# First-layer tiles of one chunk each, and the first weights ahead of the second chunk's data

## Chip, core and metric

The kernel runs on one NeuronCore of a Trainium2 chip. The metric is the device time of one execution in microseconds (us); the time before is 581.92 us, the median of 3 runs (579.84 to 582.04).

## What is computed

A scan attention over 4 batches, 8 heads, 768 positions, head size 32 and state size 16, then two feed-forward layers on the 3072 tokens of 256 features that come out of it. The scan keeps a state per batch and head; within a chunk it is a masked product of C, B and the decays:

```python
M = einsum(C, B) * L                      # L: decays between positions i >= j
y = einsum(M, x) + einsum(C, state) * decay_to_i
state = decay_full * state + sum(B * x * decay_from_j)
...
h = max(max(x @ w1, x @ w2), x @ w3)      # 256 -> 768
x = h @ w_out                             # 768 -> 256
gate = 1 / (1 + exp(-(x @ w_gate)))       # 256 -> 1536
out = gate * (x @ w_val) @ w_out2         # 1536 -> 256
```

## The kernel before, in words

The sequence is cut into 8 chunks of `CH` = 96 positions. A chunk of all 4 batches is `CP` = 384 tokens. One attention step (`attention`, L269) handles 4 of the 32 (batch, head) units of one chunk, so a chunk takes 8 steps and the whole scan 64. A step is a generator with stages: score matmuls into a PSUM tile (L280 or L283), the product with the decays into `mt` (L288 on GpSimd, L295 on VectorE; for even steps from 4 on L291 on ScalarE and L292 on GpSimd), then the matmuls into `y` (L301). After four steps half a chunk is split into `xt_hi` and `xt_lo` (L310, L312) and the state is transposed into the next chunk's `xs` (L316). Steps 0 to 15 (`FIRST`, the "masked" ones) use fp32 tables with a mask made on ScalarE (L275), and their score matmuls are fp32; later steps use bf16 splits of the tables (`split_bc`, L238, with the products `bi` and `cs`). `decay` (L227) runs two scans on VectorE for each pair of steps; `load_decay` (L211) fetches the data for it, 388 KB per pair, into one of 4 buffers.

The feed-forward matmuls work on tiles of `TT` = 512 tokens: for each tile t and each of 6 blocks m of 128 hidden features, `layer` (L415) makes 3 up-projections of 6 matmuls each (fp32 as hi and lo parts: 3 products for 2 halves of 256 features), and `down` (L356) follows one block later with 6 matmuls. A block is therefore 24 matmuls of up to 512 columns, each with a weight load of its own. The stages `most` and `hidden` (L392, L386) evict: a copy (L395, ScalarE), two maxima (L397, L399, VectorE), the hi cast (L388, ScalarE) and the lo part (L390, GpSimd). `psu` has three PSUM banks, shared by up-projections and scores.

Weights come as 64-bit floats. `load_weights` (L121) issues two transfers of 256 KB per piece on SP's queue (the second part of a second-layer piece: one), and `decode` (L130) turns a piece into hi and lo parts: three ScalarE instructions (L141, L143, L144), two VectorE (L148, L150), a cast on ScalarE (L155) and a subtraction on GpSimd (L157). The first layer has 12 pieces. `BEHIND` says how many pieces follow the issue of decay n.

The order: the prologue (L431 to L456) issues the first loads and traces `START` = 12 attention steps; then the first layer runs tile by tile, and `slot_end` (L463) traces further steps so that `need(t + 1)` of them are done before tile t + 1. Before the change need is 12, 24, 32, 44, 56, 64. The first-layer output of tile 5 is followed by the second layer's (tile, block) list. `tc.issue_after(i)` puts the instructions of its block behind i on i's engine. Each engine executes its queue in order; a scheduler of the compiler fixes that order beforehand from simulated times. All transfers are issued by SP. Per chunk there are 768 KB of x and B (`load_x`, L219), a table of 448 KB (L241 or L443) and, from chunk 2 on, 1344 KB of products (L252).

Of the kernel before, what the change touches and what calls it, by code (L numbers as in the profile page):

```python
# [7 lines left out]
F32 = mybir.dt.float32  # L8
F32R = mybir.dt.float32r
# [9 lines left out]
CH = 96  # L19
# [4 lines left out]
NT = NB * S  # L24
TT = 512
NTT = NT // TT
DM = NH * D
KD = DM // 128
FF1, FF2 = 768, 1536
# [8 lines left out]
TERMS = [(0, 0), (0, 1), (0, 2), (1, 0), (1, 1), (2, 0)]  # L38
KT = 16 * len(TERMS)
DEC = 512  # L40
START = 12
FIRST = 2 * NG
MASKED = 8
LEAD = 2
MTS = 5
DECS = 4

BEHIND = {4: 1, 5: 1, 6: 2, 7: 2, 8: 2, 9: 1, 10: 1, 11: 1, 12: 1}


class Pipe:
# [15 lines left out]
def scan_attention_then_ffn(ctx: ExitStack, tc: tile.TileContext, xh, ah, bch, pick, bn, w1, w2, w3,  # L67
# [170 lines left out]
    def split_bc(c):  # L238

        r = awk.tile([128, BW + 384], F32, tag="bc", bufs=1, name=f"bc{c}")  # L240
        sp.dma_start(out=r, in_=bch[:, c])  # L241
        parts = awk.tile([128, 3, BW + 384], BF16, tag="parts", bufs=1, name=f"parts{c}")
        cs[c] = awk.tile([KT, NU, CH], BF16, tag="cs", name=f"cs{c}")
        yield
        for p in range(3):
            with tc.issue_after(evict[0].ins) if c > 2 else ExitStack():
                act.copy(parts[:, p], r)
            for k, (dst, cols) in enumerate(((bi[c % 2], slice(0, BW)),
                                             (cs[c], slice(BW, BW + 384)))):
                for t, pr in enumerate(TERMS):  # L250
                    if pr[k] == p:
                        sp.dma_start(  # L252
                            out=dst[16 * t:16 * t + 16].rearrange("n (g q) i -> n g (q i)", q=4),
                            in_=parts[:, p, cols])
            if p < 2:
                pool.tensor_tensor(out=r, in0=r, in1=parts[:, p], op=ALU.subtract)
            yield splits if p == 2 else None
# [6 lines left out]

    def need(t):

        return 4 * -(-(t + 1) * TT // (2 * CH))

    def attention(k, ahead):  # L269

        c, g = steps[k]
        m = mt[k % MTS]
        if k < FIRST:
            ck = cm[:, k % MASKED]
            act.mul(ck.rearrange("p q i -> p (q i)"), bcf[c][:, BW:], pk[:, g:g + 1])  # L275
        ps = psu.tile([128, 4, 128], F32, tag="up", name=f"s{c}_{g}")
        for q in range(4):
            u = 4 * g + q
            if k < FIRST:
                pe.matmul(ps[:, q, 0:CH], bcf[c][:, 128 * q:128 * q + 128], ck[:, q],  # L280
                          start=True, stop=True)
            else:
                pe.matmul(ps[:, q, 0:CH], bi[c % 2][:, u, :], cs[c][:, u, :],  # L283
                          start=True, stop=True)
        for _ in range(ahead + 1):
            yield
        dc = dec[k // 2][:, 4 * (g % 2):4 * (g % 2) + 4]
        pool.tensor_tensor(out=m[:, :, CH:CH + N], in0=bx[c][:, 4 * g:4 * g + 4, :],  # L288
                           in1=dc[:, :, CH:LW].to_broadcast([128, 4, N]), op=ALU.mult)
        if k >= 4 and k % 2 == 0:  # L290
            act.copy(m[:, :, 0:CH], ps[:, :, 0:CH])  # L291
            pool.tensor_tensor(out=m[:, :, 0:CH], in0=m[:, :, 0:CH], in1=dc[:, :, 1:LW],  # L292
                               op=ALU.mult)
        else:
            last[0] = dve.tensor_tensor(out=m[:, :, 0:CH], in0=ps[:, :, 0:CH], in1=dc[:, :, 1:LW],  # L295
                                        op=ALU.mult)
        prepare(k)
        yield
        y = ys[g // 4]
        for q in range(4):  # L300
            pe.matmul(y[32 * q:32 * q + 32, g % 4, 0:CH + N], xs[c][:, 4 * g + q, :], m[:, q, :],  # L301
                      start=True, stop=True)
        if g % 4 == 3:
            yield
            h = g // 4
            o = (c * CP + 2 * CH * h) % RING
            src = y[:, :, 0:CH].rearrange("p (b k) i -> p b k i", k=KD)
            hi, lo = (v[:, :, o:o + 2 * CH].rearrange("p k (b i) -> p b k i", b=2)
                      for v in (xt_hi, xt_lo))
            act.copy(hi, src)  # L310
            yield
            dve.tensor_tensor(out=lo, in0=src, in1=hi.bitcast(F32), op=ALU.subtract)  # L312
            if c + 1 < NC:
                for q in range(4):
                    rows = slice(32 * q, 32 * q + 32)
                    dve.transpose(  # L316
                        out=xs[c + 1][rows, 16 * h:16 * h + 16, :].rearrange(
                            "p (g q) d -> p g q d", q=4)[:, :, q, :],
                        in_=y[rows, :, CH:128])

    def prepare(k):

        c, g = divmod(k, NG)
        if g == 0 and 0 < c < NC - 1:
            load_x(c + 1)
            splits.append(split_bc(c + 1))
        if splits and next(splits[0], None) is splits:
            splits.pop()
        n = k // 2
        if k % 2 == 0:  # L330
            if 5 <= n + 4 < NC * NP:
                load_decay(n + 4, ad)
        elif k < 9:
            decay(n + 1, n == 0)
        else:
            for i in ([n + 1] if k == 9 else []) + [n + 2]:
                if i < NC * NP:
                    with tc.issue_after(last[0].ins) if k > FIRST else ExitStack():
                        decay(i)

    def att_step(ahead=0):
# [12 lines left out]
    acc = {}  # L354

    def down(t, m, mn, w, hl, finish):  # L356
        if m == 0:
            acc[t] = [psos[t % len(psos)].tile([128, TT], F32, tag=f"o{d}", name=f"o{mn}_{t}_{d}")
                      for d in range(KD)]
        first = len(w) - KD  # L360
        for d in range(KD):
            three(acc[t][d], [m], mn, w, lambda k: first + d, lambda k: hl[0], lambda k: hl[1])
        if m == mn - 1:
            pipe.add(finish(t, acc[t]))

    def finish1(t, ps):
        yield
        for d in range(KD):
            act.copy(y1[:, d, t * TT:(t + 1) * TT], ps[d])

    def finish2(t, ps):
        yield
# [39 lines left out]
        chain.tick()  # L412
        pipe.tick()

    def layer(t, m, w, n, stages):  # L415

        o = (t * TT) % RING
        s = tmpp.tile([128, TT], F32, tag="s", bufs=3, name=f"s{n}_{t}_{m}")
        hl = [tmpp.tile([128, TT], F32R, tag=h, name=f"{h}{n}_{t}_{m}") for h in ("hi", "lo")]
        banks = []  # L420
        for j in range(n):
            ps = psu.tile([128, TT], F32, tag="up", name=f"u{n}_{t}_{m}_{j}")
            three(ps, range(KD), KD, w, lambda k: KD * j + k,
                  lambda k: xt_hi[:, k, o:o + TT], lambda k: xt_lo[:, k, o:o + TT])
            banks.append(ps)
            if j == 0:
                chain.add(stages(s, banks, hl))
            yield hl
# [9 lines left out]
    next(store_all, None)  # L438
    load_x(0, slice(0, 16))
    load_decay(1, ah)  # L440
    load_decay(2, ad)
    load_x(0, slice(16, 32))
    sp.dma_start(out=bcf[1], in_=bch[:, 1])  # L443
    load_decay(3, ad)
    load_x(1, slice(0, 16))
    load_decay(4, ad)
    decay(0, clip=True)
# [15 lines left out]

    def slot_end():
        t, s = divmod(slot, slots)
        if t + 1 < NTT:
            goal = need(t) + (need(t + 1) - need(t)) * (s + 1) / (slots - 5)
            while done[0] < min(goal, need(t + 1)):
                for _ in range(2 if t > 1 else 1):
                    att_step(1 if t > 1 else 0)  # L470
        tick()
        weights_tick(t < NTT - 1 or s % 3 == 2)

    for t in range(NTT):
        for m in range(M1):
            for hl in layer(t, m, wt1[m], 3, most):
                slot_end()
                slot += 1
            if pend is not None:
                down(*pend)  # L480
            slot_end()
            slot += 1
            pend = (t, m, M1, wt1[m], hl, finish1)
            if t == NTT - 1 and m == 0:
                actx.close()
                wp2.append(ctx.enter_context(tc.tile_pool(name="wp2", bufs=1)))
                psos.append(ctx.enter_context(tc.tile_pool(name="pso2", bufs=1, space=PSUM)))
                todo += [(piece2, m, part) for m in range(M2) for part in range(2)]
                while todo:
                    load_weights()  # L490
            if t == NTT - 1 and m in (2, 4):
                pipe.add(split_y(m // 2 - 1))


# [1 line left out]
    order += [(t, m) for t in range(2, NTT) for m in range(M2)]  # L496
    for t, m in order:
        eng = pool if t < 2 else dve
        for hl in layer(t, m, wt2[m], 2, lambda s, b, h: gated(s, b, h, eng)):
            tick()  # L500
            slot += 1
            weights_tick(slot % 3 == 2)
# [77 lines left out]
```

## Time and profile before

| | |
|---|---|
| median of the runs | 581.92 us |
| the profiled execution's own time | 582.93 us |
| its span, first to last instruction | 581.1 us |
| first matmul of the first layer | 38.19 us |
| first matmul of its second tile | 91.95 us |
| first matmul of the second layer | 281.42 us |
| busy: TensorE, VectorE, ScalarE, GpSimd | 560.9, 312.7, 260.7, 197.8 us |

The span begins with the first instruction of any engine and ends with the last; the rest of the execution's time lies around it. PE is TensorE's matmuls, PEld its weight loads, DVE VectorE, ACT ScalarE, POOL GpSimd, SP SyncE. Recorded matmuls overlap each other, so the pace of a stream of them is the distance of their starts, not the recorded duration.

### The profile page before, as it was taken

Reading aid. Unit: us, or ns where it says so; the run is one execution under the profiler, and the core shown is the slowest. Engines: PE = TensorE matmul, PEld = TensorE weight load, DVE = VectorE, ACT = ScalarE, POOL = GpSimd, SP = SyncE. Lnnn points to the kernel's source line nnn. Section 1 sums busy time; section 2 is a strip of 40 time slices with the busy share of each in tenths; the row PEclk is TensorE's granted clock in tenths of the full one; section 3 lists DMA queues with packets and bytes.
Section 4 is the critical chain, followed back from the end, with each engine's and each line's share of the span. In section 5 each row is a group of like instructions: output and inputs, shape, how many; then the busy total and the mean of one; then the engine's idle time right before and its main releaser. Section 6 shows DMA issues by size and latency. Waiting matters only on the chain.

```text
span 581.1 us, 8016 instructions
## 1 busy us (share of the span) xinstructions
PE 560.9 (97%) x2992; PEld 448.7 (77%) x2992; DVE 312.7 (54%) x455; ACT 260.7 (45%) x475; POOL 197.8 (34%) x219
## 2 busy tenths in 40 slices
PE   4988799999999999999999999999999999999997
PEld 4766567677777777788888888888888888888885
DVE  3879995655857754345766664243343333333332
ACT  4677645225344333256967675442333233232322
POOL 3566965427556523234665555310000000000000
PEclk9998999999999999999999999999999999999999
DMA  7999876827875800395000000010000001000000
GB/s 243 335 241 259 222 153 111 174 65 134 196 162 142 156 2 0 94 363 195 2 1 2 0 2 0 1 72 1 1 7 30 1 0 38 0 1 36 1 0 36
DMA packets 35366, 50.52 MB, mean 87 GB/s; under 512 B 3456, under 2 KB 24320, under 8 KB 35328
## 3 DMA queue, kind: packets, MB, share of 16 engines
q1 hardware_dynamic: 35328, 50.02, 33.4%
q8 instruction: 23, 0.38, 0.3%
q14 instruction: 15, 0.12, 0.1%
HBM read 38.51 MB, written 3.25 MB: 72 GB/s over the span
## 4 chain that ended last, share of the span: by engine, by line
PE 87%; DMA 6%; DVE 3%; issue 1%; SPq 1%; ACT 1%; POOL 0%; DVEq 0%; ACTq 0%; POOLq 0%
PE u L350 19%; PE u L351 18%; PE u L352 18%; PE o L351 8%; PE o L350 8%; PE o L352 8%; PE s L280 3%; PE y L301 3%; DMA raw_a<-in_w 3%; PE s L283 1%; DMA dec<-in_ah 1%; DMA cs<-parts 1%; DMA raw_a<-in_wo 1%; DVE dec L235 1%; SPq L252 0%
## 5 line engine op out<-in xcount | busy, mean ns | idle before, releaser
L388 ACT CAST hi<-s 128x512 fp32r<-128x512 f32 x108 | 67.1, 621 | 181.1 <-DVE s L406 132.1
L390 POOL TENSOR_TENSOR lo<-s,hi 128x512 fp32r<-128x512 f32 x60 | 80.9, 1348 | 95.3 <-ACT hi L388 92.3
L350 PE MATMUL u<-xt_hi,w_b 128*128 128x512 f32 x288 | 112.0, 389 | 0.0
L351 PE MATMUL u<-xt_lo,w_b 128*128 128x512 f32 x288 | 112.0, 389 | 0.0
L352 PE MATMUL u<-xt_hi,w_b 128*128 128x512 f32 x288 | 112.0, 389 | 0.0
L406 DVE TENSOR_TENSOR s<-u,s 128x512 f32<-128x512 f32 x72 | 49.6, 689 | 103.8 <-PE u L352 101.7
L350 PE MATMUL u<-xt_hi,w_a 128*128 128x512 f32 x216 | 89.1, 413 | 2.9 <-DVE s L399 2.0
L351 PE MATMUL u<-xt_lo,w_a 128*128 128x512 f32 x216 | 85.5, 396 | 0.1
L352 PE MATMUL u<-xt_hi,w_a 128*128 128x512 f32 x216 | 85.0, 394 | 0.0
L352 PEld LDWEIGHTS u<-xt_hi,w_b 128*128 128x128 f32 x288 | 54.1, 188 | 11.3
L350 PEld LDWEIGHTS u<-xt_hi,w_b 128*128 128x128 f32 x288 | 54.1, 188 | 11.2
L351 PEld LDWEIGHTS u<-xt_lo,w_b 128*128 128x128 f32 x288 | 54.0, 188 | 11.2
L235 DVE TENSOR_TENSOR_SCAN dec<-dec,delta 128x388 f32<-128x388 f32 x64 | 57.9, 945 | 1.7 <-DMA dec<-ad 1.5
L351 PE MATMUL o<-lo,w_b 128*128 128x512 f32 x144 | 56.1, 390 | 0.0
L352 PE MATMUL o<-hi,w_b 128*128 128x512 f32 x144 | 56.0, 389 | 0.0
L350 PEld LDWEIGHTS u<-xt_hi,w_a 128*128 128x128 f32 x216 | 41.2, 191 | 14.7 <-DVE s L399 2.5
L390 DVE TENSOR_TENSOR lo<-s,hi 128x512 fp32r<-128x512 f32 x48 | 33.2, 692 | 32.5 <-ACT hi L388 32.4
L352 PEld LDWEIGHTS u<-xt_hi,w_a 128*128 128x128 f32 x216 | 41.1, 190 | 9.1
L351 PEld LDWEIGHTS u<-xt_lo,w_a 128*128 128x128 f32 x216 | 41.1, 191 | 8.3 <-DVE xt_lo L312 0.6
L404 ACT ACTIVATE s<-u 128x512 f32<-128x512 f32 x72 | 43.1, 599 | 3.6 <-PE u L352 3.0
L350 PE MATMUL o<-hi,w_b 128*128 128x512 f32 x144 | 44.4, 390 | 0.1
L397 DVE TENSOR_TENSOR s<-u,s 128x512 f32<-128x512 f32 x36 | 24.8, 688 | 35.7 <-PE u L352 32.8
(60 smaller groups left out, 769.7 us busy)
## 6 DMA issues: line engine op xcount, KB each, us to landing
dec<-ad SPq DMA_DIRECT2D x30, 388.0 KB, 5.2
raw_a<-in_w SPq DMA_DIRECT2D x18, 256.0 KB, 7.2
bi<-parts SPq DMA_DIRECT2D x36, 128.0 KB, 5.3
cs<-parts SPq DMA_DIRECT2D x36, 96.0 KB, 5.2
xs<-in_xh SPq DMA_DIRECT2D x6, 512.0 KB, 4.5
raw_b<-in_wg SPq DMA_DIRECT2D x12, 256.0 KB, 5.8
raw_b<-in_wv SPq DMA_DIRECT2D x12, 256.0 KB, 5.8
raw_b<-in_wo SPq DMA_DIRECT2D x12, 256.0 KB, 5.8
```

The costliest lines, as they stand in the source:

```text
L235: dve.tensor_tensor_scan(out=f, data0=f, data1=delta.rearrange("p u w -> p (u w)"), initial=0.0, op0=ALU.mult, op1=ALU.add)
L280: pe.matmul(ps[:, q, 0:CH], bcf[c][:, 128 * q:128 * q + 128], ck[:, q], start=True, stop=True)
L283: pe.matmul(ps[:, q, 0:CH], bi[c % 2][:, u, :], cs[c][:, u, :], start=True, stop=True)
L301: pe.matmul(y[32 * q:32 * q + 32, g % 4, 0:CH + N], xs[c][:, 4 * g + q, :], m[:, q, :], start=True, stop=True)
L350: pe.matmul(ps, wlo, a_hi(k), start=k == 0, stop=False)
L351: pe.matmul(ps, whi, a_lo(k), start=False, stop=False)
L352: pe.matmul(ps, whi, a_hi(k), start=False, stop=k == kn - 1)
L388: act.copy(hl[0], s)
L390: eng.tensor_tensor(out=hl[1], in0=s, in1=hl[0].bitcast(F32), op=ALU.subtract)
L397: dve.tensor_tensor(out=s, in0=banks[1], in1=s, op=ALU.max)
L404: evict[0] = act.activation(out=s, in_=banks[0], func=AF.Sigmoid)
L406: evict[1] = dve.tensor_tensor(out=s, in0=banks[1], in1=s, op=ALU.mult)
```

## The change

The first layer runs over 7 tiles: four of 384 tokens (a chunk each) and three of 512. `need` becomes 8, 16, 24, 32, 44, 56, 64, and `START` 8. `load_weights` is called once after the load of decay 2 and once after the second chunk's table, so the first piece stands ahead of that table, of decays 3 and 4 and of the second chunk's x; `BEHIND` places the other ten pieces behind decays 4 to 9. Chunk 0's second half of x is issued before decay 2. ScalarE's casts in `split_bc` stand behind its latest eviction for every chunk, and that eviction can now be one of the attention's copies. Scans from step 11 on stand behind the latest mask product. From tile 3 on (before: tile 2) attention steps come in pairs. The second layer keeps its tiles of 512.

```diff
--- before.py
+++ after.py
@@ -24,6 +24,9 @@
 NT = NB * S
 TT = 512
 NTT = NT // TT
+
+TILES = [(CP * c, CP) for c in range(4)] + [(4 * CP + TT * c, TT) for c in range(3)]
+NT1 = len(TILES)
 DM = NH * D
 KD = DM // 128
 FF1, FF2 = 768, 1536
@@ -38,14 +41,14 @@
 TERMS = [(0, 0), (0, 1), (0, 2), (1, 0), (1, 1), (2, 0)]
 KT = 16 * len(TERMS)
 DEC = 512
-START = 12
+START = 8
 FIRST = 2 * NG
 MASKED = 8
 LEAD = 2
 MTS = 5
 DECS = 4
 
-BEHIND = {4: 1, 5: 1, 6: 2, 7: 2, 8: 2, 9: 1, 10: 1, 11: 1, 12: 1}
+BEHIND = {4: 1, 5: 1, 6: 2, 7: 2, 8: 2, 9: 2}
 
 
 class Pipe:
@@ -243,7 +246,7 @@
         cs[c] = awk.tile([KT, NU, CH], BF16, tag="cs", name=f"cs{c}")
         yield
         for p in range(3):
-            with tc.issue_after(evict[0].ins) if c > 2 else ExitStack():
+            with tc.issue_after(evict[0].ins):
                 act.copy(parts[:, p], r)
             for k, (dst, cols) in enumerate(((bi[c % 2], slice(0, BW)),
                                              (cs[c], slice(BW, BW + 384)))):
@@ -264,7 +267,7 @@
 
     def need(t):
 
-        return 4 * -(-(t + 1) * TT // (2 * CH))
+        return 4 * -(-sum(TILES[t]) // (2 * CH))
 
     def attention(k, ahead):
 
@@ -288,7 +291,7 @@
         pool.tensor_tensor(out=m[:, :, CH:CH + N], in0=bx[c][:, 4 * g:4 * g + 4, :],
                            in1=dc[:, :, CH:LW].to_broadcast([128, 4, N]), op=ALU.mult)
         if k >= 4 and k % 2 == 0:
-            act.copy(m[:, :, 0:CH], ps[:, :, 0:CH])
+            evict[0] = act.copy(m[:, :, 0:CH], ps[:, :, 0:CH])
             pool.tensor_tensor(out=m[:, :, 0:CH], in0=m[:, :, 0:CH], in1=dc[:, :, 1:LW],
                                op=ALU.mult)
         else:
@@ -307,7 +310,7 @@
             src = y[:, :, 0:CH].rearrange("p (b k) i -> p b k i", k=KD)
             hi, lo = (v[:, :, o:o + 2 * CH].rearrange("p k (b i) -> p b k i", b=2)
                       for v in (xt_hi, xt_lo))
-            act.copy(hi, src)
+            evict[0] = act.copy(hi, src)
             yield
             dve.tensor_tensor(out=lo, in0=src, in1=hi.bitcast(F32), op=ALU.subtract)
             if c + 1 < NC:
@@ -331,11 +334,12 @@
             if 5 <= n + 4 < NC * NP:
                 load_decay(n + 4, ad)
         elif k < 9:
-            decay(n + 1, n == 0)
+            with tc.issue_after(last[0].ins) if k > 9 else ExitStack():
+                decay(n + 1, n == 0)
         else:
             for i in ([n + 1] if k == 9 else []) + [n + 2]:
                 if i < NC * NP:
-                    with tc.issue_after(last[0].ins) if k > FIRST else ExitStack():
+                    with tc.issue_after(last[0].ins) if k > 9 else ExitStack():
                         decay(i)
 
     def att_step(ahead=0):
@@ -354,8 +358,9 @@
     acc = {}
 
     def down(t, m, mn, w, hl, finish):
+        n = hl[0].shape[1]
         if m == 0:
-            acc[t] = [psos[t % len(psos)].tile([128, TT], F32, tag=f"o{d}", name=f"o{mn}_{t}_{d}")
+            acc[t] = [psos[t % len(psos)].tile([128, TT], F32, tag=f"o{d}", name=f"o{mn}_{t}_{d}")[:, 0:n]
                       for d in range(KD)]
         first = len(w) - KD
         for d in range(KD):
@@ -366,7 +371,8 @@
     def finish1(t, ps):
         yield
         for d in range(KD):
-            act.copy(y1[:, d, t * TT:(t + 1) * TT], ps[d])
+            o, n = TILES[t]
+            act.copy(y1[:, d, o:o + n], ps[d])
 
     def finish2(t, ps):
         yield
@@ -412,16 +418,18 @@
         chain.tick()
         pipe.tick()
 
-    def layer(t, m, w, n, stages):
-
-        o = (t * TT) % RING
-        s = tmpp.tile([128, TT], F32, tag="s", bufs=3, name=f"s{n}_{t}_{m}")
-        hl = [tmpp.tile([128, TT], F32R, tag=h, name=f"{h}{n}_{t}_{m}") for h in ("hi", "lo")]
+    def layer(tile, m, w, n, stages):
+
+        o, size = tile
+        name = f"{n}_{o}_{m}"
+        r = slice(o % RING, o % RING + size)
+        s = tmpp.tile([128, TT], F32, tag="s", bufs=3, name=f"s{name}")[:, 0:size]
+        hl = [tmpp.tile([128, TT], F32R, tag=h, name=f"{h}{name}")[:, 0:size] for h in ("hi", "lo")]
         banks = []
         for j in range(n):
-            ps = psu.tile([128, TT], F32, tag="up", name=f"u{n}_{t}_{m}_{j}")
+            ps = psu.tile([128, TT], F32, tag="up", name=f"u{name}_{j}")[:, 0:size]
             three(ps, range(KD), KD, w, lambda k: KD * j + k,
-                  lambda k: xt_hi[:, k, o:o + TT], lambda k: xt_lo[:, k, o:o + TT])
+                  lambda k: xt_hi[:, k, r], lambda k: xt_lo[:, k, r])
             banks.append(ps)
             if j == 0:
                 chain.add(stages(s, banks, hl))
@@ -438,10 +446,12 @@
     next(store_all, None)
     load_x(0, slice(0, 16))
     load_decay(1, ah)
+    load_x(0, slice(16, 32))
     load_decay(2, ad)
-    load_x(0, slice(16, 32))
+    load_weights()
+    load_decay(3, ad)
     sp.dma_start(out=bcf[1], in_=bch[:, 1])
-    load_decay(3, ad)
+    load_weights()
     load_x(1, slice(0, 16))
     load_decay(4, ad)
     decay(0, clip=True)
@@ -463,17 +473,17 @@
 
     def slot_end():
         t, s = divmod(slot, slots)
-        if t + 1 < NTT:
+        if t + 1 < NT1:
             goal = need(t) + (need(t + 1) - need(t)) * (s + 1) / (slots - 5)
             while done[0] < min(goal, need(t + 1)):
-                for _ in range(2 if t > 1 else 1):
-                    att_step(1 if t > 1 else 0)
+                for _ in range(2 if t > 2 else 1):
+                    att_step(1 if t > 2 else 0)
         tick()
-        weights_tick(t < NTT - 1 or s % 3 == 2)
-
-    for t in range(NTT):
+        weights_tick(t < NT1 - 1 or s % 3 == 2)
+
+    for t in range(NT1):
         for m in range(M1):
-            for hl in layer(t, m, wt1[m], 3, most):
+            for hl in layer(TILES[t], m, wt1[m], 3, most):
                 slot_end()
                 slot += 1
             if pend is not None:
@@ -481,14 +491,14 @@
             slot_end()
             slot += 1
             pend = (t, m, M1, wt1[m], hl, finish1)
-            if t == NTT - 1 and m == 0:
+            if t == NT1 - 1 and m == 0:
                 actx.close()
                 wp2.append(ctx.enter_context(tc.tile_pool(name="wp2", bufs=1)))
                 psos.append(ctx.enter_context(tc.tile_pool(name="pso2", bufs=1, space=PSUM)))
                 todo += [(piece2, m, part) for m in range(M2) for part in range(2)]
                 while todo:
                     load_weights()
-            if t == NTT - 1 and m in (2, 4):
+            if t == NT1 - 1 and m in (2, 4):
                 pipe.add(split_y(m // 2 - 1))
 
 
@@ -496,7 +506,7 @@
     order += [(t, m) for t in range(2, NTT) for m in range(M2)]
     for t, m in order:
         eng = pool if t < 2 else dve
-        for hl in layer(t, m, wt2[m], 2, lambda s, b, h: gated(s, b, h, eng)):
+        for hl in layer((t * TT, TT), m, wt2[m], 2, lambda s, b, h: gated(s, b, h, eng)):
             tick()
             slot += 1
             weights_tick(slot % 3 == 2)
```

## Rows read from the trace of the kernel before

**Rows 1.** section 1 of the page: busy us (share) and instructions

```profile
PE 560.9 (97%) x2992; PEld 448.7 (77%) x2992; DVE 312.7 (54%) x455; ACT 260.7 (45%) x475; POOL 197.8 (34%) x219
```

**Rows 2.** by stage: us; PE, PEld, DVE, ACT, POOL busy; clock, DMA, GB/s

```profile
8.40:38.19 29.79, 27.02 (x186) 22.36 (x186) 24.51 (x39) 17.23 (x31) 13.92 (x22) 1.00 0.94 289
38.19:91.95 53.76, 47.53 (x298) 34.77 (x299) 49.74 (x71) 33.28 (x59) 38.28 (x38) 0.97 0.89 220
91.95:281.42 189.47, 188.73 (x1202) 145.77 (x1201) 107.14 (x176) 79.42 (x144) 88.66 (x99) 1.00 0.56 133
211.14:248.78 37.64, 37.64 (x242) 28.96 (x241) 16.20 (x25) 12.16 (x23) 12.73 (x14) 1.00 0.18 54
248.78:281.42 32.64, 32.64 (x146) 27.03 (x145) 15.82 (x26) 20.66 (x42) 14.22 (x11) 1.00 0.68 229
```

**Rows 3.** waits of PE up to 92 us; then a piece of the chain

```profile
PE s L280 <- DMA y<-in_bch: 6.7, 1, 6.7
PE u L350 <- DVE s L399: 1.6, 1, 1.6
PE s L283 <- DVE s L399: 1.6, 1, 1.6
...
52.93 5.79 DMA raw_a<-in_wo
```

**Rows 4.** timeline of PE: start us, us, instruction, count

```profile
15.14 2.02 PE L280 MATMUL s<-y 128*128 128x96 f32 x8
...
17.63 2.02 PE L280 MATMUL s<-y 128*128 128x96 f32 x8
...
41.79 0.63 PE L352 MATMUL u<-xt_hi,w_a 128*128 128x512 f32 x1
42.22 0.63 PE L350 MATMUL u<-xt_hi,w_a 128*128 128x512 f32 x1
...
43.91 0.39 PE L351 MATMUL u<-xt_lo,w_a 128*128 128x512 f32 x1
44.13 0.39 PE L352 MATMUL u<-xt_hi,w_a 128*128 128x512 f32 x1
44.36 1.02 PE L280 MATMUL s<-y 128*128 128x96 f32 x8
45.17 0.48 PE L350 MATMUL u<-xt_hi,w_a 128*128 128x512 f32 x1
```

**Rows 5.** timeline of PE, then of PEld, around 112 us

```profile
112.12 0.39 PE L351 MATMUL u<-xt_lo,w_a 128*128 128x512 f32 x1
...
111.77 0.19 PEld L350 LDWEIGHTS u<-xt_hi,w_a 128*128 128x128 f32 x1
111.88 0.19 PEld L351 LDWEIGHTS u<-xt_lo,w_a 128*128 128x128 f32 x1
112.12 0.19 PEld L352 LDWEIGHTS u<-xt_hi,w_a 128*128 128x128 f32 x1
```

**Rows 6.** groups of DVE up to 92 us: count | busy us, mean ns

```profile
L235 DVE TENSOR_TENSOR_SCAN dec<-dec,delta 128x388 f32<-128x388 f32 x28 | 25.4, 946 | 1.7 <-DMA dec<-ad 1.5
L148 DVE SCALAR_TENSOR_TENSOR t_a<-raw_a,sg 128x512 int32<-128x512 int32 x12 | 13.3, 1111 | 1.2 <-DMA cs<-parts 1.1
L150 DVE CUSTOM_DVE_ANT_0 r_a<-t_a,r_a 128x1024 uint16<-128x1024 uint16 x12 | 13.1, 1095 | 0.8 <-ACT raw_a L143 0.5
L295 DVE TENSOR_TENSOR mt<-s,dec 128x384 f32<-128x384 f32 x14 | 7.6, 546 | 2.9 <-PE s L280 2.9
L316 DVE STREAM_TRANSPOSE xs<-y 32x128 f32<-32x128 f32 x24 | 7.4, 310 | 0.2
...
L399 DVE TENSOR_TENSOR s<-u,s 128x512 f32<-128x512 f32 x5 | 3.4, 679 | 0.1
```

**Rows 7.** timeline: last first-layer weights, their issue (SP) and last decode (POOL)

```profile
67.86 0.33 SPq L127 DMA_DIRECT2D raw_a<-in_wo  x1
...
85.27 1.28 POOL L157 TENSOR_TENSOR w_a<-r_a,w_a 128x512 fp32r<-128x512 f32 x1 [2.34 <-ACT w_a L155]
```

## Prediction

> **What bounds the kernel now.** I read the busy shares first: TensorE works for 97% of the span [rows 1], so most of what can be won is either TensorE work that gets cheaper or the little time in which it waits. The table by stage comes next. Its edges are the first matmuls of the first layer (38.19 us), of that layer's second tile (91.95), and of the second layer (281.42) [rows 2]. From 91.95 to 281.42 TensorE is busy for 188.73 of 189.47 us: nothing waits there. From 38.19 to 91.95 it is busy for 47.53 of 53.76 us, and VectorE for 49.74, which is 92.5% of the stretch [rows 2]. So during the first tile VectorE's queue is the fullest. The waits and the chain say the same: TensorE stands 1.6 us twice for a VectorE maximum (L399), and behind that the chain runs through weight transfers of 5.79 us and the like [rows 3]: VectorE executes in order, and a decode instruction that is late holds up the eviction behind it. The DMA engines are busy for 0.94 and 0.89 of the two early stretches [rows 2].
>
> One more thing in the rows: TensorE starts slow. Eight masked score matmuls and what follows them repeat every 2.49 us at 15.14; at 44.36 the same eight lengthen the stream by 45.17 - 44.13 - 0.23 = 0.81 us. First-layer matmuls stand 0.43 us apart from 41.79 to 42.22 and 0.22 us apart from 43.91 to 44.13 [rows 4]. These are the two levels, 1.2 and 2.4 GHz. (The clock column shows 1.00 before 43 us; the spacings contradict it there.) TensorE reached the upper level some 5 us after the first layer began. What runs before that costs double.
>
> **The change, part by part.** Everything is counted against the profiled execution: span 581.10 us, its own time 582.93, so 1.83 lie around the span; the median of the runs, 581.92, is 1.0 below it.
>
> *First matmul of the first layer.* Twelve attention steps stand ahead of it now, eight afterwards. At 2.49 us each [rows 4] the four taken away are 10 us of slow TensorE work. Eight steps end at about 6.7 (the first score matmul, which waits for its table [rows 3]) + 8 x 2.49 + about 1 for two waits = 27.5 us, and the split of chunk 0 needs another 1 to 2. The first weights, issued some 5 us earlier on SP's queue, have 2 to 3 MB fewer in front of them (chunk 1's x, the second tables, chunk 2's table): at 289 GB/s [rows 2] that is 7 to 9 us earlier. They still have to pass ScalarE, VectorE and GpSimd. I take 30 us for the first matmul (between 28, where the attention allows it, and 35, where the decode would still be late).
> What the weights are moved past: chunk 1's table and x are needed by step 8, now after 30 us, so 1 MB of delay (3.5 us) is covered; decay 3 had about as many bytes ahead of it before. Four issues on SP at about 0.4 us each are covered by transfers that are longer.
>
> *The first tile.* TensorE's own work from 30 us: 18 x 6 + 5 x 6 = 138 matmuls of 384 columns, eight masked steps at 0.81 plus the price of an ordinary second half (a whole ordinary step costs (37.64 - 32.64) / 8 = 0.625 us [rows 2]), so about 1.3 each, and 2.4 us for the slow clock of the first 5 us. A matmul of 512 columns takes 32.64 / 144 = 226.7 ns [rows 2]; 512 columns at 2.4 GHz are 213.3, so 13.4 are over. If they are fixed, 384 columns take 160 + 13.4 = 173.4; if they grow with the columns, 170.0. I take 173.4, the dearer. Sum: 23.9 + 10.4 + 2.4 = 36.7, end at 66.7 us.
> VectorE needs longer. From 8.4 to 91.95 us it works 24.51 + 49.74 = 74.3 us [rows 2]. With 16 steps instead of 24 in that time fall away: 8 of 28 scans (7.6), 4 of 14 mask products (2.2), 8 of 24 transposes (2.5), 2 splits (1.1 at 0.55), and 11 maxima that shrink from 0.68 to about the 0.55 of a 384-wide operation (1.4) [rows 6]. 14.8 less leaves 59.5. The 24 decode operations of 1.1 us stay. By 30 us, at the present rate of 24.51 in 29.79 us from 8.4 on, 17.8 are done; 41.7 remain. At 92.5% busy that ends at 75.1, at 100% at 71.7. I take the middle, 73.4.
> The weights agree: the last ones are now issued at 67.86 and decoded at 86.6 [rows 7]. The transfers of eight attention steps no longer stand ahead of them: four decays of 388 KB, one chunk's x of 768, table of 448 and products of 1344, together 4.1 MB, at 220 GB/s [rows 2] some 18 us. So they are decoded at about 68, and only the last third of a block needs them.
>
> *From the second tile on.* Three tiles of 384: 3 x 144 x 0.1734 = 74.9. Three of 512: 3 x 32.64 = 97.9. Attention now leaves 48 steps to this stretch, not 40: 48 x 0.625 = 30.0. Waits and rest as now: 189.47 - 5 x 32.64 - 40 x 0.625 = 1.3. Second layer unchanged: 581.1 - 281.42 = 299.7 [rows 2]. Sum 503.8. The narrower tiles alone cost 576 x 13.4 - 432 x 13.4 ns = 1.9 us of this and the first tile (0 if the 13.4 ns grow with the columns).
>
> *Orders.* Splits of later chunks behind the latest ScalarE eviction, and scans behind the last mask product from step 11: nothing, since bi and cs are needed one chunk later and scans run two pairs ahead. Without that cover, one scan (0.95 us [rows 6]) once or twice, in the first tile.
>
> **Sum:** 73.4 + 503.8 = 577.2 us of span, 3.9 less; 579.0 for the profiled execution. On the median that is **578.0 us**. Each microsecond by which the first tile ends earlier or later moves it by one.
>
> **A rule of the skill against it.** The rows show a 384-column stream nowhere. They show that a weight load begins together with the preceding matmul (both at 112.12), and that two loads can follow each other after 0.11 us (111.77, 111.88), though each is recorded with 0.19 [rows 5]; 0.11 is well below 0.173, so the load stays hidden. The Trainium skill, "TensorE: Matmul & The Clock Gate", Part 3, "The mechanism", says that a load overlaps running matmuls only if it uses another row group; all loads here use all rows, and its section on LDWEIGHTS gives 107 ns for 128 columns. By that rule 144 further loads would add an estimated 15.4 us and the change would lose. The rows speak against it, since the load at 112.12 runs beside a matmul.
>
> **The rivals.**
> *TensorE alone decides (0.20).* If earlier weights let VectorE work without holes and ahead, the first tile ends at 66.7 to 70 us: 571.3 to 574.6. For it: VectorE idled 5.3 us between 8.4 and 38.19 [rows 2]. Against: its 59.5 us from 8.4 on end at 67.9 at the very best.
> *The queues hold as before (0.17).* The first weights land little earlier, because the transfers ahead of them fill the DMA engines anyway, or a decode instruction stands at the head of VectorE's queue and waits; the first matmul then comes at 33 to 36 and the tile ends at 77.5 to 80: 582 to 584.6. For it: DMA at 0.94 [rows 2]; the change then does only half of what it says.
> *Narrow blocks outrun their evictions (0.10).* A block of 24 matmuls shrinks from 5.44 to 4.16 us, while score tiles share the same three PSUM banks. The tile with 12 steps gives VectorE some 25 us of work in 32.5. If each of 24 blocks waits 0.3 us: 7 more, 584 to 586.
> *Slower: the load sets the spacing (0.08).* Place: every 384-column matmul of tiles 2 to 4, 432 in number. At the recorded 0.19 plus a few ns the spacing is 191, not 173: 7.6 us more, 585.5; at today's 227 it is 23 more, 601. It decides from 189 ns on (below, the 3.9 us of gain keep the time within 0.5%). For it: no row with fewer columns. Against: the 0.11 us between loads.
>
> **How the numbers follow.** My case, first tile ending at 71 to 77 (575.6 to 581.6), gets 0.45. About 0.5% (2.9 us) is what a measurement of this kernel can tell from no change. Faster: two thirds of my case and the first rival, 0.30 + 0.20 = 0.50. Same: the rest of my case and most of the second rival, 0.15 + 0.15 = 0.30. Slower: 0.02 + 0.10 + 0.08 = 0.20. From 570.5 to 586 the range takes in the first three rivals and leaves out nearly all of the last.
>
> **What would show it.** First u matmul near 30 us; u matmuls of 384 columns 173 ns apart, 170 if the excess grows with the columns, 190 or more if loads bind; first masked step after the clock rise at about 0.8 us; second tile starting at 71 to 77; VectorE above 90% busy until then; tiles 2 to 4 at 30.0, 30.0 and 32.5 us without waits for L397 or L399. A second tile after 78, or waits in tiles 2 to 4, proves me wrong.

## The result and the profile after

The changed kernel takes 584.11 us (median of 10 runs, 581.24 to 584.94); the kernel before, on the same chip, 580.86 (10 runs, 579.08 to 582.04). The ratio is 1.0052, 95% interval 1.0036 to 1.0067: slower by half a per cent, where 0.7% faster was forecast (578.0 against the 581.92 known then, range 570.5 to 586). The profiled execution of before, on which the sum was built, was a long one: 582.93 against that median, 2.1 us above it. That of after is typical: 584.35, span 582.6.

The table by stage of the changed kernel; the edges are the first matmuls of tiles 1, 2, 3, 4 and 5 of the first layer, the last row runs from the second tile to the second layer. Columns as in [rows 2].

```profile
8.40:28.03 19.63, 11.89 (x121) 9.68 (x121) 16.73 (x27) 12.11 (x24) 7.74 (x14) 0.83 1.00 362
28.03:73.41 45.38, 40.11 (x267) 34.90 (x267) 43.77 (x60) 31.26 (x57) 33.40 (x32) 0.92 0.73 201
73.41:104.55 31.14, 31.14 (x242) 27.04 (x241) 19.57 (x36) 11.83 (x24) 15.74 (x20) 1.00 0.67 136
104.55:135.69 31.14, 31.14 (x242) 26.97 (x241) 18.85 (x34) 11.81 (x24) 15.72 (x20) 1.00 0.66 137
135.69:172.22 36.53, 32.60 (x286) 29.75 (x286) 24.95 (x45) 15.38 (x30) 22.28 (x28) 0.95 0.90 173
...
73.41:282.88 209.47, 205.54 (x1441) 170.77 (x1441) 122.58 (x210) 87.65 (x167) 100.67 (x119) 0.99 0.61 141
```

Read it against [rows 2]. The first layer starts at 28.03 and its second tile at 73.41: of the first part of the forecast (30 and 73.4) the start came 2 us earlier and the end as summed, VectorE filling 43.77 of 45.38 us. The loss is in the last row: 209.47 us where 204.1 were summed. Tiles 2 and 3 take 31.14 each (forecast 30.0) with TensorE busy throughout. The fourth takes 36.53 (forecast 32.5); there TensorE is idle for 3.9 us, the granted clock falls to 0.95 and DMA is at 0.90.

The waits of PE from 73 to 283 us, all of them:

```profile
PE s L286 <- DMA dec<-ad: 3.9, 1, 3.9
```

The timeline of PE around that wait (L286 is the bf16 score matmul, L354 to L356 the first layer's):

```profile
152.29 0.33 PE L356 MATMUL u<-xt_hi,w_a 128*128 128x384 f32 x1
152.46 0.33 PE L354 MATMUL u<-xt_hi,w_a 128*128 128x384 f32 x1
152.63 0.33 PE L355 MATMUL u<-xt_lo,w_a 128*128 128x384 f32 x1
152.81 0.34 PE L356 MATMUL u<-xt_hi,w_a 128*128 128x384 f32 x1
157.07 0.33 PE L286 MATMUL s<-cs,bi 96*128 96x96 bf16 x4 [3.92 <-DMA dec<-ad]
...
158.88 0.52 PE L354 MATMUL u<-xt_hi,w_a 128*128 128x384 f32 x1
159.20 0.52 PE L355 MATMUL u<-xt_lo,w_a 128*128 128x384 f32 x1
```

The table by stage for the time after the wait, columns as above:

```profile
157.94:161.35 3.41, 3.41 (x14) 3.41 (x15) 2.93 (x5) 1.52 (x3) 3.25 (x4) 0.50 0.65 195
```

Two things stand in them. From 152.29 to 152.81 three matmuls of 384 columns start 0.52 / 3 = 0.173 us apart: the forecast spacing; the loads bind nothing. After the wait they start 0.32 apart until about 161.4: from 157.94 to 161.35, 3.4 us, the granted clock is 0.50, the lower level, 1.2 GHz. So the wait costs 3.9 us and then more; with the tile of 31.03 us found below for the same steps without a wait, 36.53 - 31.03 - 3.9 = 1.6.

The timeline of SP in the fourth tile, where chunk 5's last product (`cs`, L255) is issued, with the DMA view of that issue and of the decay issued behind it (KB, us to landing), and two rows of VectorE (L238 is the scan of a decay, L405 the second maximum of a block):

```profile
146.27 0.33 SPq L216 DMA_DIRECT2D dec<-ad  x1
...
147.73 0.56 SPq L255 DMA_DIRECT2D bi<-parts  x1
148.35 0.58 SPq L255 DMA_DIRECT2D cs<-parts  x1
149.40 0.33 SPq L216 DMA_DIRECT2D dec<-ad  x1
...
cs<-parts SPq DMA_DIRECT2D x1, 96.0 KB, 8.3
dec<-ad SPq DMA_DIRECT2D x1, 388.0 KB, 8.0
...
154.52 1.81 DVE L238 TENSOR_TENSOR_SCAN dec<-dec,delta 128x388 f32<-128x388 f32 x2 [3.44 <-DMA dec<-ad]
156.25 0.53 DVE L405 TENSOR_TENSOR s<-u,s 128x384 f32<-128x384 f32 x1
```

148.35 + 8.3 = 156.65, just ahead of 157.07. The steps of tile 4 are 32 to 43, and step 40 opens chunk 5: its score matmul is the first to read these products. The view of waits names a decay instead, and the chain of work the one issued at 149.40. It can't be that one: it landed at 157.4, when the matmul had begun. But a decay is late too: VectorE's scan stands 3.44 us for the one issued at 146.27, and the maximum behind it ends only at 156.78. So the products and VectorE were ready within 0.2 us of each other, and this trace alone can't tell which of them held TensorE. That, and what else the change costs, is for the experiments.

### The profile page after: what moved, and what is told of

It is laid out like the page before. It is cut to its first block, busy times and chain, and to the rows that moved or that the text cites. A ratio compares the mean times of both kernels' runs of the same rounds, so it can differ in the third digit from the quotient of the medians.

```text
span 582.6 us, 8347 instructions
## 1 busy us (share of the span) xinstructions
PE 555.2 (95%) x3136; PEld 461.3 (79%) x3136; DVE 314.6 (54%) x467; ACT 262.2 (45%) x489; POOL 199.3 (34%) x225
## 4 chain that ended last, share of the span: by engine, by line
PE 85%; DMA 10%; DVE 1%; SPq 1%; ACT 1%; issue 1%; DVEq 0%; ACTq 0%
PE u L354 19%; PE u L356 19%; PE u L355 19%; PE o L355 8%; PE o L354 8%; PE o L356 8%; DMA raw_a<-in_w 4%; DMA dec<-ad 2%; PE y L304 2%; PE s L286 2%; DMA cs<-parts 1%; DMA bi<-parts 1%; SPq L255 1%; DMA ad<-ac 1%; DVE t_a L151 0%
## 5 line engine op out<-in xcount | busy, mean ns | idle before, releaser
L394 ACT CAST hi<-s 128x512 fp32r<-128x512 f32 (+1 forms) x114 | 68.0, 597 | 184.0 <-DVE s L412 132.9
L396 POOL TENSOR_TENSOR lo<-s,hi 128x512 fp32r<-128x512 f32 (+1 forms) x66 | 82.9, 1257 | 93.4 <-ACT hi L394 92.1
L354 PE MATMUL u<-xt_hi,w_b 128*128 128x512 f32 x288 | 112.0, 389 | 0.0
L356 PE MATMUL u<-xt_hi,w_b 128*128 128x512 f32 x288 | 112.0, 389 | 0.0
L412 DVE TENSOR_TENSOR s<-u,s 128x512 f32<-128x512 f32 x72 | 49.7, 690 | 109.2 <-PE u L356 105.8
L354 PE MATMUL u<-xt_hi,w_a 128*128 128x384 f32 (+1 forms) x252 | 95.8, 380 | 4.4 <-POOL w_a L160 1.7
L355 PE MATMUL u<-xt_lo,w_a 128*128 128x384 f32 (+1 forms) x252 | 91.9, 365 | 0.6 <-DVE xt_lo L315 0.6
L356 PE MATMUL u<-xt_hi,w_a 128*128 128x384 f32 (+1 forms) x252 | 91.6, 364 | 0.0
L354 PEld LDWEIGHTS u<-xt_hi,w_b 128*128 128x128 f32 x288 | 54.1, 188 | 11.2
L356 PEld LDWEIGHTS u<-xt_hi,w_b 128*128 128x128 f32 x288 | 54.0, 188 | 11.2
L238 DVE TENSOR_TENSOR_SCAN dec<-dec,delta 128x388 f32<-128x388 f32 x64 | 57.9, 944 | 4.6 <-DMA dec<-ad 4.2
L354 PEld LDWEIGHTS u<-xt_hi,w_a 128*128 128x128 f32 x252 | 48.4, 192 | 13.0 <-issue 2.9
L356 PE MATMUL o<-hi,w_b 128*128 128x512 f32 x144 | 56.0, 389 | 0.0
L355 PEld LDWEIGHTS u<-xt_lo,w_a 128*128 128x128 f32 x252 | 48.5, 192 | 5.0 <-DVE xt_lo L315 1.0
L356 PEld LDWEIGHTS u<-xt_hi,w_a 128*128 128x128 f32 x252 | 48.3, 192 | 4.4
L403 DVE TENSOR_TENSOR s<-u,s 128x384 f32<-128x384 f32 (+1 forms) x42 | 25.6, 609 | 36.4 <-PE u L356 35.0
L354 PE MATMUL o<-hi,w_b 128*128 128x512 f32 x144 | 44.6, 390 | 0.1
```

What stands on the lines that cost most here:

```text
L238: dve.tensor_tensor_scan(out=f, data0=f, data1=delta.rearrange("p u w -> p (u w)"), initial=0.0, op0=ALU.mult, op1=ALU.add)
L354: pe.matmul(ps, wlo, a_hi(k), start=k == 0, stop=False)
L355: pe.matmul(ps, whi, a_lo(k), start=False, stop=False)
L356: pe.matmul(ps, whi, a_hi(k), start=False, stop=k == kn - 1)
L394: act.copy(hl[0], s)
L396: eng.tensor_tensor(out=hl[1], in0=s, in1=hl[0].bitcast(F32), op=ALU.subtract)
```

## Experiments

The ratios are to the kernel before, run on the same chips beside each kernel; the changed kernel has 1.0052.

**The steps spread evenly.**

```diff
-        return 4 * -(-sum(TILES[t]) // (2 * CH))
+        return (8, 16, 26, 36, 44, 56, 64)[t]
```

> Edit of the changed kernel: the steps due before tiles 3 and 4 are 26 and 36 (not 24 and 32), so the fourth tile, of 384 columns, is given 8 steps in place of 12 and the second and third 10 each. Theory A (the late decay: in the fourth tile the scan of a pair two pairs ahead stands at the head of VectorE's queue until its transfer lands, the maximum L405 behind it is late, TensorE stands 3.9 us and then runs 3.4 us at the lower clock): no wait of TensorE above 1 us between 73 and 283 us, the fourth tile at about 30 us in place of 36.5, some 5 us less in all, 578.5 to 579.5 us, ratio to before 0.996 to 0.998. Theory B (the price is in the narrow tiles themselves, each step costing 0.77 us there): no gain, 583 to 585, ratio 1.004 to 1.007, with the loss spread over tiles 2 to 4.

578.45 us, ratio 0.9966 (0.9953 to 0.9978). No wait of PE is left between 73 and 277 us, and the fourth tile, now with 8 steps, reads

```profile
136.83:166.56 29.73, 29.73 (x242) 27.26 (x242) 19.24 (x36) 11.81 (x23) 15.58 (x20) 1.00 0.75 163
```

By the ratios the kernel is 5.0 us faster than the changed one. B falls as the main cause: the loss sits in the tile with 12 steps, not in narrow tiles as such. A's number came out, but any transfer that is late in that tile would give it.

**Scans one pair ahead.**

```diff
-            for i in ([n + 1] if k == 9 else []) + [n + 2]:
+            for i in ([n + 1, n + 2] if k == 9 else [n + 2] if k < 25 else [n + 1] if k > 25 else []):
```

> Edit of the changed kernel: from step 25 on the scans run one pair ahead of their step, not two. The steps per tile, the transfers and their order stay as traced. Theory A (a scan whose transfer has not landed blocks VectorE's queue): the scan that waited at about 152.8 us is needed some 10 us later, so the 3.9 us wait and the low clock after it go, 578.5 to 579.5 us, ratio 0.996 to 0.998. Theory C (the fourth tile's transfers are simply too many for its 32 us): the wait moves to the step that needs the scan, at least 2 us of it stay, 582 to 585.

582.70 us, ratio 1.0035 (1.0020 to 1.0049). The wait of PE in the fourth tile stays:

```profile
PE s L286 <- DMA dec<-ad: 3.0, 1, 3.0
...
147.94 0.59 SPq L255 DMA_DIRECT2D cs<-parts  x1
...
152.33 0.53 DVE L405 TENSOR_TENSOR s<-u,s 128x384 f32<-128x384 f32 x1
...
155.74 0.33 PE L286 MATMUL s<-cs,bi 96*128 96x96 bf16 x4 [2.98 <-DMA dec<-ad]
...
cs<-parts SPq DMA_DIRECT2D x1, 96.0 KB, 7.7
```

Theory A in this form is refuted: a scan that stands too early in VectorE's queue explains at most 0.9 of the 3.9 us. VectorE waits for no decay in this tile, and its maximum ends at 152.86; TensorE stands until 155.74 all the same. The last product lands at 147.94 + 7.7 = 155.6. So the products alone hold TensorE for 3.0 us.

**Five decay buffers.**

```diff
-DECS = 4
+DECS = 5
```

> Edit of the changed kernel: five buffers for the decays, not four, so a decay's transfer waits one pair of steps less for its buffer. Theory A with the buffer as the reason why the transfer is late: decay transfers of the fourth tile are issued 3 us or more earlier, ahead of some of the chunk's products, the wait of 3.9 us shrinks below 1 us, 578.5 to 580 us. Theory C (the queue of products ahead of it makes it late, not the buffer): the wait stays above 2 us, 582 to 585. The order in the first tile changes too, by 1 us at most in either direction.

583.51 us, ratio 1.0041 (1.0024 to 1.0059). The view of waits now names another transfer:

```profile
PE s L286 <- DMA bi<-parts: 2.5, 1, 2.5
```

So the decays are not what comes last; a product is. This led to theory D. The wait is 1.4 us shorter, but the second tile starts 1.05 us later than in the changed kernel, at 74.46, and the time hardly changes.

**Chunk 5's products begun two steps earlier.**

```diff
-            splits.append(split_bc(c + 1))
+            if c != 4:
+                splits.append(split_bc(c + 1))
+        if k == 30:
+            splits.append(split_bc(5))
```

> Edit of the changed kernel: chunk 5's bf16 products (casts, transfers into bi and cs) are begun at step 30, not 32; the steps per tile stay 8, 8, 8, 12, 12, 8. Theory D (the late products: with 12 steps in a 384-column tile, step 40 opens chunk 5 when its last product transfer, issued at 148.35 and landing at 156.6, is not there; TensorE's score matmul at 157.07 waits for it, and neither the scan two pairs ahead nor the decay's buffer is the cause): the products land some 6 us earlier, the wait falls below 0.5 us, no low clock after it, 578.5 to 579.5 us, ratio to before 0.996 to 0.998. Theory A (the decay transfer behind the scan): the decays stand behind the same number of transfers, the wait stays above 2 us, 582 to 584.

578.25 us, ratio 0.9964 (0.9950 to 0.9977), with the 12 steps still in the fourth tile, which starts at 135.06 here. Its row, and the issue of the last product:

```profile
135.06:166.09 31.03, 31.03 (x285) 28.10 (x285) 24.77 (x45) 14.51 (x29) 20.35 (x27) 1.00 0.81 184
...
142.74 0.59 SPq L255 DMA_DIRECT2D cs<-parts  x1
```

The last product is issued 7.7 us into the tile, not 12.7, and TensorE does not wait at all. D's ratio came out (0.996 to 0.998; the time is 0.25 us under its range); A gave 582 or more. One reservation: the decays come earlier too (VectorE waits for none here), so the run shows that products begun earlier remove the wait, not that late decays alone could never cause one.

**The orders undone.** Casts and scans are ordered as in the kernel before.

```diff
-            with tc.issue_after(evict[0].ins):
+            with tc.issue_after(evict[0].ins) if c > 2 else ExitStack():
...
-            evict[0] = act.copy(m[:, :, 0:CH], ps[:, :, 0:CH])
+            act.copy(m[:, :, 0:CH], ps[:, :, 0:CH])
...
-            evict[0] = act.copy(hi, src)
+            act.copy(hi, src)
...
-                    with tc.issue_after(last[0].ins) if k > 9 else ExitStack():
+                    with tc.issue_after(last[0].ins) if k > FIRST else ExitStack():
```

> Edit of the changed kernel: the orders alone are undone (product casts stand behind an eviction only from chunk 3 on and behind the first layer's evictions only, scans behind the mask product only after step 16). If the orders make chunk 5's products late (a cast that waits for an eviction of the attention): the wait of 3.9 us in the fourth tile shrinks below 2 us, 580 to 582 us, ratio 0.998 to 1.002. If they are worth nothing, as the prediction has it: wait of 3 to 5 us, 583 to 585, ratio 1.004 to 1.007.

581.43 us, ratio 1.0010 (0.9999 to 1.0020): 2.4 us better than the changed kernel by the ratios, so the orders are not free. The run undoes both at once; what each of them costs is not shown. The second and third tile (72.80 and 103.35) are shorter and the wait is halved:

```profile
72.80:103.35 30.55, 30.55 (x242) 27.08 (x242) 18.92 (x34) 11.73 (x24) 15.72 (x20) 1.00 0.68 139
103.35:133.90 30.55, 30.55 (x242) 27.07 (x242) 18.91 (x34) 11.73 (x24) 15.71 (x20) 1.00 0.69 139
...
PE s L286 <- DMA cs<-parts: 1.9, 1, 1.9
```

Here the view names `cs` itself.

**Pairs from the second tile on.**

```diff
-                for _ in range(2 if t > 2 else 1):
-                    att_step(1 if t > 2 else 0)
+                for _ in range(2 if t > 0 else 1):
+                    att_step(1 if t > 0 else 0)
```

> Edit of the changed kernel: attention steps come in pairs from the second tile on, not from the fourth on. Theory B (steps one by one cost 0.77 us in a tile, in pairs 0.56 to 0.63, because the y matmuls of two steps then share one break of the stream): tiles 2 and 3 go from 31.1 to about 30.0 us each, 2 us less in all; with the wait in the fourth tile untouched 581.5 to 582.5 us, ratio 1.001 to 1.003. If the price per step is none of the pairing: no change, 583.5 to 584.5.

580.76 us, ratio 0.9995 (0.9980 to 1.0011). Tiles 2 and 3, from 72.75 on, keep their 8 steps:

```profile
72.75:102.36 29.61, 29.61 (x237) 26.62 (x237) 18.94 (x36) 11.56 (x23) 15.68 (x20) 1.00 0.72 143
102.36:132.60 30.24, 30.24 (x241) 27.34 (x241) 18.72 (x35) 11.69 (x23) 15.75 (x20) 1.00 0.68 141
```

2.4 us less for the two, as expected; a wait of 2.5 us stays in the fourth tile. It is 1.4 shorter than in the changed kernel, and so the ratio is below the expected 1.001 to 1.003; why it is shorter is open.

**Both together**, the even spread and the pairs (the two diffs above).

> Edit of the changed kernel: both the even distribution of the steps (8, 10, 10, 8, 12, 8) and pairs from the second tile on. If the two effects are separate (5.5 us from the wait and the clock after it, 2 to 3 us from the pairs): 575 to 576.5 us, ratio 0.990 to 0.993, and no wait of TensorE above 1 us between 73 and 278 us. If ten steps in pairs in a narrow tile bring the wait back there: 578 to 581.

575.64 us, ratio 0.9924 (0.9907 to 0.9942): the effects are separate and add up, and this kernel beats both. **With the orders undone on top:**

> Edit of the changed kernel: the even distribution (8, 10, 10, 8, 12, 8), pairs from the second tile on, and the orders undone as in the run on the orders. If the orders cost time only by making chunk 5's products late and by the single steps of tiles 2 and 3, nothing is left for them here: 575 to 577 us, ratio 0.990 to 0.993, as with the two other edits alone. If they cost something in every tile: 573 to 574.5 us, ratio 0.986 to 0.990.

576.03 us, ratio 0.9919 (0.9901 to 0.9937), the same within the intervals. Once neither single steps nor late products are there, the orders cost nothing.

**The first weights back behind decays 4 and 5.**

```diff
     load_decay(2, ad)
-    load_weights()
     load_decay(3, ad)
     sp.dma_start(out=bcf[1], in_=bch[:, 1])
-    load_weights()
...
-BEHIND = {4: 1, 5: 1, 6: 2, 7: 2, 8: 2, 9: 2}
+BEHIND = {4: 2, 5: 2, 6: 2, 7: 2, 8: 2, 9: 2}
```

> Edit of the changed kernel: the first two pieces of weights go back behind decays 4 and 5 (two pieces behind each), so behind the second chunk's table and x; tiles of 384 and eight first steps stay. If the load order is what lets the first layer start at 28 us: first u matmul at 33 to 36, second tile at 77 to 80, 588 to 591 us with the wait in the fourth tile untouched, ratio 1.011 to 1.017. If the first tile's end is set by VectorE's amount of work alone: second tile at 73 to 75 all the same, 584 to 586.

587.73 us, ratio 1.0122 (1.0087 to 1.0157). The first first-layer matmul waits for the weights' last decode step (L160) for 3.8 us (in the changed kernel it stands 1.1 us, by the view of waits for a transfer of weights):

```profile
32.62 0.69 PE L354 MATMUL u<-xt_hi,w_a 128*128 128x384 f32 x1 [3.79 <-POOL w_a L160]
```

It comes 4.6 us later and the second tile, at 76.68, 3.3 us later: the tile's length hardly changes (44.06 against 45.38, VectorE busy for 41.64), as when VectorE's work sets it. The second tile comes between the two expectations, nearer to the first, and the wait in the fourth tile stays, with 3.4 us.

**Tiles of 512 and twelve first steps, with the new load order.** The orders stay as changed, too.

```diff
-TILES = [(CP * c, CP) for c in range(4)] + [(4 * CP + TT * c, TT) for c in range(3)]
+TILES = [(TT * c, TT) for c in range(6)]
...
-START = 8
+START = 12
...
-                for _ in range(2 if t > 2 else 1):
-                    att_step(1 if t > 2 else 0)
+                for _ in range(2 if t > 1 else 1):
+                    att_step(1 if t > 1 else 0)
```

> Edit of the changed kernel: six tiles of 512 and twelve first steps as before; the new load order, BEHIND and the orders by eviction stay. If the load order alone gave the gain of the first tile: the second tile starts 4 us or more before 91.95, 576 to 578 us, ratio 0.990 to 0.996. If the gain needs the first layer to start after eight steps (the weights were not the last to come): second tile at 90 to 92 and 580 to 582 us, ratio 0.998 to 1.003.

582.31 us, ratio 1.0031 (1.0018 to 1.0043). The first tile runs from 36.63 to 90.86, where [rows 2] have 38.19 to 91.95:

```profile
36.63:90.86 54.23, 48.32 (x299) 35.56 (x299) 49.11 (x69) 31.60 (x55) 40.54 (x39) 1.00 0.80 190
```

The second tile starts 1.1 us earlier than in [rows 2], but those come from the long execution, and against the runs this kernel is 0.3% slower. Earlier weights show no gain as long as twelve steps stand ahead of the first layer (the run keeps the orders, so it does not show what the load order costs by itself), and with eight first steps late weights lose 4 us by the ratios (1.0122 against 1.0052). The gain of the first tile needs both halves of the change.

## Why the prediction was wrong

**Right.** The first layer's start (28.03, said 30), VectorE as what sets the first tile's end (96% busy; 16.73 + 43.77 = 60.5 us of work, said 59.5; argued from these shares, as no run takes work off VectorE alone), the second tile's start (73.41, said 73.4), the spacing of 384 columns (0.173). That 73.4 was met to the hundredth is luck: the first layer started 2.0 us earlier, and its first tile took 2.0 us longer (45.38 against 43.4). The second layer took 582.6 - 282.9 = 299.7 us, as said. The sentence of the Trainium skill that loads overlap running matmuls only if the row groups differ ("TensorE: Matmul & The Clock Gate", Part 3, "The mechanism") disagrees with this trace: all loads here use all rows, and with it the spacing could not be 0.173 beside loads recorded with 0.19. The same section also lets a load into the background weight buffer go ahead; whether that is what happens here, no run shows.

**The step that failed: "From the second tile on".** It gave 503.8 us; it took 5.4 more, the whole error of the span (582.6 against 577.2). One of the prediction's own signs of being wrong came: a wait in tiles 2 to 4. The terms:
- *The tile with 12 steps.* It was priced as TensorE work alone, 12 x 0.625 + 25.0 = 32.5; it took 36.5. What was not asked is whether the data come in time when the same 12 steps share 32 us, not the 32.64 + 12 x 0.625 = 40.1 of a 512-column tile [rows 2]. Step 40 opens chunk 5, whose products are begun with step 33 in the same tile; the last landed 21 us into it, and TensorE waited 3.9 us and ran slowly for 3.4. With VectorE out of the way 3.0 of the 3.9 stayed (scans one pair ahead), and the matmul began 0.1 us after the last product. Spreading the steps, or starting the products earlier, removed all of it and made the kernel faster than before (0.9966, 0.9964). The rival "narrow blocks outrun their evictions" had the right tile but the wrong cause: the view has no wait for a maximum after 73 us, and the one maximum that was late there stood behind a scan that waited for its decay.
- *The price of a step.* 0.625 came from a tile of [rows 2] in which steps come in pairs. The change moves the begin of the pairs from the third to the fourth tile, so tiles 2 and 3 have single steps: (31.14 - 24.97) / 8 = 0.77. Two tiles: 2.3 us. Pairs gave it back. The trace of before has a tile with single steps, its second:

  ```profile
  91.95:130.16 38.21, 38.21 (x238) 27.77 (x237) 20.92 (x36) 13.34 (x23) 17.37 (x20) 1.00 0.56 111
  ```

  (38.21 - 32.64) / 8 = 0.70, and 0.70 is also the price without the orders, (30.55 - 24.97) / 8. So about half of the 2.3 is the price of single steps, which a row of before had, and half is what the orders add to them.
- *The orders,* put at nothing and hidden by "one chunk later". In this kernel that cover was gone in the fourth tile: undoing them brought the last product earlier, halved the wait, and took 0.6 us off each of tiles 2 and 3. They are worth 2.4 us, part of the two terms above.
- *Against it:* the three tiles of 512 took 110.7 us, 1.1 less than their share of the sum, since the 1.3 of "waits and rest" hardly came.

**The base.** The profiled execution of before was 2.1 us above the median that the result was measured against. A gain of 3.9 us counted from it is one of 1.8, or 0.3%, against the median, so the sum did not carry a forecast of "faster by over 0.5%". Without the wait the ratio is 0.9964, short of that too; with the steps spread and paired as well it is 0.9924, more than was summed.

## What to carry to other kernels

If work is cut into smaller tiles with the same schedule, price not only each tile's compute but also the data that the tile must receive: the same number of transfers in less time, and who first reads the last of them. A schedule in "steps per tile" has to be redrawn when the tiles change. Take the price of a unit from rows with the same arrangement (single or paired), and test a base profile against the spread of the runs before building a gain of half a per cent on it.

## What was not expected of the hardware

In the execution shown of before the masked steps ran at the lower level of the clock ([rows 4], 2.49 us per step). In the one shown of the changed kernel the clock reaches its upper level after the first three (their 24 score matmuls take 5.10 us from 6.54 on, the eight at 12.39 take 1.10): from 13.76 to 15.15 one step takes 1.39 us. By the start of the first layer it is down again, at 0.50 (the row at 28.52).

```profile
13.76 1.13 PE L283 MATMUL s<-y 128*128 128x96 f32 x8
...
15.15 1.13 PE L283 MATMUL s<-y 128*128 128x96 f32 x8
...
28.52 1.85 PE L283 MATMUL s<-y 128*128 128x96 f32 x8
```

The first layer did not start earlier for it: in the even-spread kernel the same steps repeat every 2.49 us, and its first layer starts at 27.80.

```profile
15.07 2.02 PE L283 MATMUL s<-y 128*128 128x96 f32 x8
...
17.56 2.02 PE L283 MATMUL s<-y 128*128 128x96 f32 x8
```

Both first layers stand 1.1 us for a transfer of weights first, by the view of waits, so it was not the pace of the masked steps that held them. And the wait of 3.9 us was followed by 3.4 us at the lower clock, in the middle of a stream that had been dense for 80. The length of a wait does not settle it: in the kernel with five decay buffers a wait of 2.5 us in the fourth tile was followed by no fall (granted clock 1.00 over the whole tile); with pairs from the second tile on a wait of 2.5 us was followed by one (0.95).
